# Windowed attention and a feed-forward layer on one core: how Q and K loads, V loads and token blocks are lined up

## The chip, the cores and the metric

The kernel runs on one core of a Trainium2 chip. Its engines work side by side, each with its own in-order list of instructions: TensorE (PE, with its weight loads shown apart as PEld), VectorE (DVE), ScalarE (ACT), GpSimd (POOL) and SyncE (SP), which here issues all DMA transfers. The metric is the device time of one execution in microseconds (us); lower is better.

## The reference

```python
def _attn_ref(q, k, v):                      # all (8, 8, 576, 64): batch, head, token, dim
    scores = (1.0 / np.sqrt(64)) * np.matmul(q, k.transpose(0, 1, 3, 2))
    mask = np.abs(pos[:, None] - pos[None, :]) <= 32
    scores = np.where(mask, scores, -1000000000.0)
    attn = np.exp(scores - np.max(scores, axis=-1, keepdims=True))
    attn = attn / (np.sum(attn, axis=-1, keepdims=True) + 1e-09)
    return np.matmul(attn, v)

def _moe_ref(x, w_in, w_out, s, b):          # x (4608, 512), w_in (512, 2048), w_out (2048, 512)
    r = np.maximum(x @ w_in, 0.0)
    return (s * (r * r) + b) @ w_out         # out (4608, 512), float32
```

Attention within 32 tokens on either side, for 8 batches of 8 heads, gives 8 x 576 = 4608 rows of 512, and each row goes through a layer of 2048 hidden values.

## The kernel before, in words

**One graph, ordered by a planner.** The kernel records every piece of work as a task with `add`: the engine, the instructions, an assumed cost, what it reads and writes, a key (its due time), and for a transfer a triple `dma=(kind, units, ns per unit)`. `_Graph.plan` then plays the tasks through with these costs: at each step it takes, over all engines, the task that can start first (ties go to the smaller key), and keeps a model of SP's DMA ring, in which transfers are served one after another. The order in which it takes the tasks becomes the fixed order of each engine, and `emit` puts the semaphore waits in. So a changed cost, wait or due time does not only move one instruction: it can reorder all engines, and at run time an engine whose next instruction has to wait lets everything behind it wait.

**Attention.** Batches 0 and 1 are loaded and turned in a special way. From batch 2 on (`later`, `piece`) each batch has three loads on SP's queue (line 752): 512 tokens of Q (1 MB), 512 tokens of K (1 MB), and the last 64 tokens of both together. Each lands in a pair of staging buffers `stg` and is cast to bf16 `nat` in two halves (line 760); from batch 3 on, half 0 is POOL's and half 1 DVE's. DMA transposes (line 767) then bring `nat` to `qt` and `ktr`, and POOL copies `ktr` to `kt` in the order wanted (line 777). V comes in units of 128 tokens (`load_v`, line 582, into `vst`) and is cast to `vb` (`cast_v`, line 591, on DVE from batch 2 on). A batch is 4.5 such units. For unit u, PE makes the scores (line 811), ACT the exponentials `ex` (839), DVE multiplies them by the mask (843), PE multiplies by V one unit later, with the row sums (869), in one step together with the next unit's scores, DVE takes reciprocals `rec` (893) and makes the normalised rows `xn` (895), and PE (902) with ACT (910), or later in the kernel a DMA transpose (919), bring these to `xt`, the input of the layer.

What paces the loads: `paced(b, u)` makes a load of batch b wait until a certain attention step of an earlier batch is done. Besides that, the Q and K loads of batch 3 and later wait until the last V load of the batch before has landed (lines 792 and 793).

**The layer.** The 4608 tokens are cut into blocks (`sizes`, line 341): 224, 128, 160, 256, 256 and then 512 each. For each block, `s1` (lines 1113 to 1135) multiplies by `w_in` (PE, line 1124), applies ReLU on ACT (1131) and squares on DVE into `gt` (1133). A group of `s1` fills one accumulator of 512 columns: one chunk of hidden values for a block of 512, two for a block of 256 (`group`). `s2` (line 1142) multiplies 128 tokens of `gt` by `w_out`, in four steps of four matmuls; DVE scales the result to `outs` (1158) and SP writes it (1162). A block's squares must be ready before its `s2`; its `xt` must be ready before its `s1`. Due times of attention units (`due`) are worked out from the block in which their tokens lie, and those of the blocks from a running sum of assumed PE times.

Of the kernel before, what the change touches and what calls it, by code (L numbers as in the profile page):

```python
# [21 lines left out]
PAIRS = 2  # L22
# [25 lines left out]
PACE = ((-1, -1, -1),) * 3  # L48
CASTS = 40.0
LATE = 8  # L50
# [31 lines left out]
class _Graph:  # L82
# [13 lines left out]
    def add(self, stream, fns, cost, reads=(), writes=(), key=0.0, accum=False, dma=None, waits=(),  # L96
            lat=None, slack=0.0):
        if not isinstance(fns, list):
            fns = [fns]
        after = [self.chain] if key < -100 and self.chain else []  # L100
        t = _Task(len(self.tasks), stream, fns, cost, self.LAT[stream] if lat is None else lat, key,
                  dma, slack, after)
        t.deps.update(waits)
        for a in after:
            assert a.stream == stream
            a.next.append(t)
        for r in reads:
            assert r in self.writer, r
            t.deps.add(self.writer[r])
        for w in writes:  # L110
            if w in self.writer:
                t.deps.add(self.writer[w])
            if not accum:
                t.deps.update(self.readers.get(w, ()))
        t.deps.discard(t)
        for r in reads:
            self.readers.setdefault(r, []).append(t)
        for w in writes:
            self.writer[w] = t
            if not accum:  # L120
                self.readers[w] = []
        self.tasks.append(t)
        if key < -100:
            self.chain = t
        return t
# [201 lines left out]
def bass_sliding_window_symmetric__then__act_starrelu_kernel(  # L327
# [10 lines left out]
    B = q.shape[0]  # L338
    T = B * S

    sizes = [224, 128, 160, 256, 256]
    NE = 3
    while sum(sizes) < T:
        sizes.append(min(512, T - sum(sizes)))
# [6 lines left out]
    with ExitStack() as es:  # L351
        uid = {"n": 0}

        def seq_of(b):
            return min(b, LONG)
# [97 lines left out]
        def group_of(b):  # L453

            if b < LONG:
                return range(NUNIT)
            u0 = (NTILE * (b - LONG)) // 2
            return range(u0, (NTILE * (b + 1 - LONG) + (b == B - 1)) // 2)
# [75 lines left out]
        land = {}  # L534

        def pieces(lo, hi, step):
            return range(lo // step, (hi - 1) // step + 1)

        def take(what, n):
            ring[what] += 1  # L540
            return (ring[what] - 1) % n
# [19 lines left out]
        def paced(b, u):  # L561

            c, v = seq_of(b - 1), group_of(b - 1)[0] + u
            while v < 0:
                c, v = c - 1, v + NUNIT
            return land["av", c, v]

        def late(b):

            return "sp" if b < LATE else "act"  # L570
# [166 lines left out]
        def q_later(b):  # L737
            return QTS[b % 2].rearrange("p (i a) s -> p i a s", i=4)

        def piece(b, parts, key, waits):  # L740


            slot = b % 2
            ring["stg"] += ring["stg"] % 2
            ring["nat"] += ring["nat"] % 2
            si, _ = take("stg", NSTG), take("stg", NSTG)
            ni, _ = take("nat", NNAT), take("nat", NNAT)
            stg = STGS[:, si:si + 2, :].rearrange("p x c -> p (x c)")
            nat = NATS[:, ni:ni + 2, :].rearrange("p x c -> p (x c)")
            stgr, natr = [("STG", si), ("STG", si + 1)], [("NAT", ni), ("NAT", ni + 1)]  # L750
            top = max(p0 + n // 4 for _, _, n, p0 in parts)
            add(late(b), [lambda e, name=name, t0=t0, n=n, p0=p0: e.dma_start(
                stg[p0:p0 + n // 4, :].rearrange("p (h c) -> p h c", h=H),
                src_of[name][b, :, t0:t0 + n, :].rearrange("h (p i) d -> p h (i d)", i=4))
                for name, t0, n, p0 in parts],
                500.0 * len(parts), writes=stgr, key=key - 20.0, waits=waits,
                dma=("l", sum(n for _, _, n, _ in parts) // 8, 68.0 if late(b) == "sp" else 61.0))
            for x in (0, 1):
                eng = CASTE[min(b, 3) - 2][x]
                add(eng, lambda e, x=x: e.tensor_copy(  # L760
                    nat[0:top, 1024 * x:1024 * x + 1024].rearrange("p (i h d) -> p h i d", h=H, i=2),
                    stg[0:top, :].rearrange("p (h i d) -> p h i d", h=H, i=4)[:, :, 2 * x:2 * x + 2, :]),
                    110 + (0.53 if eng == "dve" else 1.05) * 1024, reads=stgr, writes=[("NAT", ni + x)], key=key + CASTS, slack=SLACK[0])
            for name, t0, n, p0 in parts:
                np_, s0, xs = n // 4, t0 // 4, pieces(t0, t0 + n, 64)
                dst = q_later(b)[:, :, :, 16 + s0:16 + s0 + np_] if name == "q" else KTR[slot][:, :, :, s0:s0 + np_]
                add("sp", lambda e, dst=dst, p0=p0, np_=np_: e.dma_start(
                    dst.rearrange("p i a s -> p (i a) s"), nat[p0:p0 + np_, :], transpose=True),
                    2000.0 if n > 64 else 1200.0, reads=natr,
                    writes=[("QT", slot, x, pr) for x in xs for pr in range(NPAIR)] if name == "q" else [("KTR", slot, t0)],  # L770
                    key=key + 0.1, dma=("t", np_, 20.0))
                if name == "q":
                    continue
                land["kt", b, t0] = g.tasks[-1]
                for c in range(t0, t0 + n, 128):
                    w = min(128, t0 + n - c)
                    add("pool", lambda e, c=c, w=w: e.tensor_copy(  # L777
                        KT[slot][:, :, c:c + w].rearrange("p a (s i) -> p a s i", i=4),
                        KTR[slot][:, :, :, c // 4:(c + w) // 4].rearrange("p i a s -> p a s i")),
                        100 + 5.5 * w, reads=[("KTR", slot, t0)],  # L780
                        writes=[("KT", slot, x, pr) for x in pieces(c, c + w, 64) for pr in range(NPAIR)],
                        key=key + 3.0, slack=SLACK[1])

        def later(b, key):
            slot = b % 2
            if b < 4:
                for c0, x in ((0, 0), (160, WIN + S)):
                    add("pool", lambda e, c0=c0: e.memset(QTS[slot][:, :, c0:c0 + 16], 0.0), 400,
                        writes=[("QTZ", slot, x)] + [("QT", slot, x, pr) for x in range(NTILE) for pr in range(NPAIR)],
                        key=key - 20.0)  # L790
            for i, parts in enumerate(((("q", 0, 512, 0),), (("k", 0, 512, 0),), (("q", 512, 64, 0), ("k", 512, 64, 32)))):
                piece(b, parts, key + 0.01 * i, [paced(b, PACE[min(b, 4) - 2][i])] +
                      ([land["v", seq_of(b - 1), group_of(b - 1)[-1]]] if b > PAIRS or LATE == PAIRS else []))

# [227 lines left out]
        def attention():  # L1024
# [60 lines left out]
            for b in range(PAIRS, B):  # L1085
                c = seq_of(b)
                later(b, due(c, group_of(b)[0]) - 24.0)
                for i, u in enumerate(group_of(b)):
                    load_v(c, u, due(c, u) - 35.0, late(b), [paced(b, PACEV[min(b, 4) - 2][i])])
                    cast_v(c, u, due(c, u) - 4.0, EV2[i], SLACK[3])  # L1090
                for u in group_of(b):
                    unit(c, u)
                    yield closed[0]
# [381 lines left out]
```

## Time and profile before

| | us |
|---|---|
| three runs | 314.92, 315.22, 316.3 |
| median | 315.22 |
| the profiled execution, its own time | 317.31 |
| its span, first to last instruction | 315.5 |
| PE busy in the span | 296.7 |
| DMA: share of 16 engines' time taken by the data queue | 75.5% |

The granted TensorE clock was 1.0 throughout. In rows of a timeline the columns are: start in us from the span's start, length in us, engine (SPq is SP's queue of DMA issues), line of the kernel, operation, what is written and read, count, and in brackets the idle time before it and what ended it. Lengths of matmuls overlap: the start of the next one tells how long PE was taken. In rows of busy time by stage, each engine's busy time is followed by its number of instructions, and the last three columns are the granted clock, the share of DMA and GB/s.

### The profile page before, as it was taken

To read this page: it belongs to the slowest core of one execution; us is meant where nothing else is said; L and a number is where in the kernel's file an instruction comes from. 1 tells how busy PE (TensorE), PEld (TensorE's weight loads), DVE (VectorE), ACT (ScalarE), POOL (GpSimd) and SP (SyncE) were. 2 spreads that over 40 slices of the span, in tenths; PEclk is the share of its full clock that TensorE was granted. 3 is DMA by queue.
4 is the path that set the end of the run, shared out by engine and by line. 5 is a ranking of instruction groups with operands and counts; after the bars stand their busy time and mean duration, and the time that the engine had idled before them with its cause. 6 is when DMAs were issued, how large, how long until landed. Compare 5 with 4: busy or idle time off the path is not lost.

```text
span 315.5 us, 7901 instructions
## 1 busy us (share of the span) xinstructions
PE 296.7 (94%) x3304; PEld 160.6 (51%) x3348; DVE 195.5 (62%) x387; ACT 141.9 (45%) x224; POOL 93.0 (29%) x110
## 2 busy tenths in 40 slices
PE   7788989999979998999999999999999999999996
PEld 3367756577734544544444444444444444444444
DVE  4678476876596777888577687766445543333312
ACT  4755425356525773654255346444444333333300
POOL 5468854671236235131613241260000000000000
PEclk9999999999999999999999999999999999999999
DMA  6999999997998998799999999996221110000022
GB/s 198 331 386 386 372 251 218 218 199 246 236 188 205 294 140 166 219 225 169 175 318 157 161 221 336 165 154 162 64 59 50 52 46 33 35 34 34 36 91 80
DMA packets 100055, 56.10 MB, mean 178 GB/s; under 512 B 72048, under 2 KB 91248, under 8 KB 100016
## 3 DMA queue, kind: packets, MB, share of 16 engines
q1 hardware_dynamic: 100016, 55.56, 75.5%
q8 instruction: 27, 0.44, 0.6%
q14 instruction: 12, 0.10, 0.1%
HBM read 36.70 MB, written 9.44 MB: 146 GB/s over the span
## 4 chain that ended last, share of the span: by engine, by line
PE 68%; DMA 19%; DVE 6%; issue 3%; SPq 2%; POOL 1%; ACT 0%; POOLq 0%
PE o L1142 30%; PE w L1124 28%; DMA stg<-in_k_dram 10%; DMA stg<-in_moe_w_out_dram 3%; PE avn L869 3%; DMA stg<-in_moe_w_in_dram 3%; DVE gt L1133 2%; PE avn L1173 2%; DMA stg<-in_q_dram 2%; PE sc L811 1%; PE o L1173 1%; DMA vst<-in_v_dram 1%; SPq L667 1%; DVE xn L895 1%; DVE nat L760 1%
## 5 line engine op out<-in xcount | busy, mean ns | idle before, releaser
L1124 PE MATMUL w<-xt,win 128*128 128x512 bf16 (+4 forms) x749 | 140.2, 324 | 3.0 <-ACT r L1131 1.4
L1131 ACT ACTIVATE r<-w 128x512 bf16<-128x512 f32 (+2 forms) x148 | 86.6, 586 | 107.1 <-PE w L1124 91.3
L1142 PE MATMUL o<-wout,gt 128*128 128x512 bf16 (+1 forms) x510 | 123.1, 372 | 2.0 <-issue 1.4
L1133 DVE TENSOR_TENSOR gt<-r 128x512 bf16<-128x512 bf16 (+2 forms) x148 | 79.9, 545 | 72.3 <-ACT r L1131 71.9
L1124 PEld LDWEIGHTS w<-xt,win 128*128 128x128 bf16 x768 | 68.3, 98 | 54.0 <-DVE kt L711 0.9
L1142 PEld LDWEIGHTS o<-wout,gt 128*128 128x128 bf16 x528 | 50.6, 98 | 54.6
L760 POOL CAST nat<-stg 128x1024 bf16<-128x1024 f32 (+1 forms) x21 | 26.7, 1271 | 60.7 <-DMA stg<-in_q_dram 37.6
L777 POOL COPY kt<-ktr 128x512 bf16<-128x512 bf16 (+1 forms) x30 | 31.6, 1054 | 38.5 <-DMA ktr<-nat 37.1
L839 ACT ACTIVATE ex<-sc 128x1024 bf16<-128x1024 f32 (+1 forms) x28 | 28.7, 1023 | 23.2 <-PE avn L869 22.4
L1158 DVE SCALAR_TENSOR_TENSOR outs<-o,sb,cvec 128x512 f32<-128x512 f32 (+1 forms) x35 | 25.4, 729 | 14.2 <-PE o L1142 14.0
L895 DVE TENSOR_TENSOR xn<-avn,rec 128x512 bf16<-128x512 f32 (+1 forms) x31 | 21.4, 689 | 1.1 <-DVE rec L893 0.2
L843 DVE TENSOR_TENSOR ex<-ex,mask 128x1024 bf16<-128x1024 bf16 (+1 forms) x28 | 21.2, 758 | 1.0 <-ACT ex L839 0.2
L869 PE MATMUL avn<-vb,ex 64*64 64x65 bf16 x944 | 19.9, 197 | 1.5 <-issue 1.3
L869 PEld LDWEIGHTS avn<-vb,ex 64*64 64x64 bf16 x944 | 12.9, 106 | 14.5 <-issue 8.7
L760 DVE CAST nat<-stg 128x1024 bf16<-128x1024 f32 (+1 forms) x15 | 11.1, 740 | 7.2 <-DMA stg<-in_k_dram 5.1
L591 DVE CAST vb<-vst 128x512 bf16<-128x512 f32 (+1 forms) x28 | 13.7, 494 | 0.0
L811 PE MATMUL sc<-qt,kt 64*64 64x128 bf16 x432 | 11.3, 216 | 0.0
L910 ACT COPY xt<-avn 128x512 bf16<-128x512 bf16 (+2 forms) x14 | 7.1, 516 | 8.1 <-PE avn L902 8.1
L893 DVE RECIPROCAL rec<-avn 128x8 f32<-128x8 f32 (+1 forms) x31 | 6.2, 201 | 5.9 <-PE avn L869 5.5
L557 POOL CAST win<-stg 128x1024 bf16<-128x1024 f32 x8 | 8.4, 1056 | 3.7 <-DMA stg<-in_moe_w_in_dram 3.6
L557 POOL CAST wout<-stg 128x1024 bf16<-128x1024 f32 x8 | 9.0, 1122 | 1.7 <-DMA stg<-in_moe_w_out_dram 1.0
L1173 PE MATMUL o<-wout,gt 128*128 128x512 bf16 x29 | 8.2, 379 | 1.0 <-POOL wout L557 0.9
(119 smaller groups left out, 146.1 us busy)
## 6 DMA issues: line engine op xcount, KB each, us to landing
out_dram<-outs SPq DMA_DIRECT2D x35, 256.0 KB, 2.5
vst<-in_v_dram SPq DMA_DIRECT2D x28, 256.0 KB, 5.2
stg<-in_k_dram SPq DMA_DIRECT2D x6, 1024.0 KB, 11.1
stg<-in_q_dram SPq DMA_DIRECT2D x6, 1024.0 KB, 6.6
stg<-in_moe_w_in_dram SPq DMA_DIRECT2D x8, 512.0 KB, 9.2
stg<-in_moe_w_out_dram SPq DMA_DIRECT2D x8, 512.0 KB, 9.6
stg<-in_q_dram SPq DMA_DIRECT2D x8, 256.0 KB, 5.4
stg<-in_k_dram SPq DMA_DIRECT2D x8, 256.0 KB, 5.4
```

The lines of the kernel that those rows point to most:

```text
L760: add(eng, lambda e, x=x: e.tensor_copy(nat[0:top, 1024 * x:1024 * x + 1024].rearrange("p (i h d) -> p h i d", h=H, i=2), stg[0:top, :].re ...
L777: add("pool", lambda e, c=c, w=w: e.tensor_copy(KT[slot][:, :, c:c + w].rearrange("p a (s i) -> p a s i", i=4), KTR[slot][:, :, :, c // 4: ...
L839: add("act", lambda e, dst=flat_dst, src=flat_src: e.activation(dst, src, AF.Exp, bias=0.0, scale=0.125), 190 + 0.833 * 512 * len(hs), rea ...
L843: add("dve", lambda e, flat=flat, mask=mask: e.tensor_tensor(flat, flat, mask, ALU.mult), 130 + 0.53 * 512 * len(hs), reads=[("E", ei, hp, ...
L869: return [lambda e: e.matmul(av[64 * x:64 * x + 64, h, 0:D + 1], lhsT=buf[64 * g:64 * g + 64, h % 2, h // 2, c:c + 64], rhs=VB[64 * g:64 * ...
L895: add("dve", lambda e: e.tensor_tensor(XN[xi][0:p1, :].rearrange("p (a c) -> p a c", a=H), av[0:p1, :, 0:D], REC[ri][0:p1, :].rearrange("p ...
L1124: add("pe", [lambda e, g=g, kc=kc: e.matmul(wt[:, g, :], lhsT=WIN_BF[:, kc, (f0 + g) * 128:(f0 + g + 1) * 128], rhs=XT[:, kc, t0 % XR:t0 % ...
L1131: add("act", lambda e: e.activation(rt, wt, AF.Relu, bias=0.0, scale=1.0), 190 + 0.833 * ng * nt, reads=[("W", wb)], writes=[("R1", rb)], ...
L1133: add("dve", lambda e: e.tensor_tensor(GT[gs][:, f0:f0 + ng, g0:g0 + nt], rt, rt, ALU.mult), 130 + 0.53 * ng * nt, reads=[("R1", rb)], wri ...
L1142: add("pe", [lambda e, fc=fc: e.matmul(O[:, ob, 0:cn], lhsT=GT[gs][:, fc, g0:g0 + 128], rhs=WOUT_BF[:, fc, c0:c0 + cn], start=(fc == 0), s ...
L1158: add("dve", lambda e: e.scalar_tensor_tensor(OUTS[us][:, 0:cn], bank, SB128[:, 0:1], CVEC[:, c0:c0 + cn], ALU.mult, ALU.add), 200 + 1.07 ...
L1173: add("pe", [lambda e, fc=fc, bank=bank, gs=gs, g0=g0: e.matmul(bank, lhsT=GT[gs][:, fc, g0:g0 + 128], rhs=WOUT_BF[:, fc, :], start=(fc == ...
```

## The change

Three edits. The block of tokens 1024 to 1535 becomes two blocks of 256, so that there are 13 blocks in place of 12. The planner counts 74 ns in place of 68 for each of the 64 units of a large Q or K load (and of the 16 of the small one). And the wait of Q and K loads for the last V load of the batch before is taken away; their pacing stays. Since lines go, the changed kernel's numbers after line 792 are one lower (869 becomes 868, 1124 becomes 1123).

```diff
-    sizes = [224, 128, 160, 256, 256]
+    sizes = [224, 128, 160, 256, 256, 256, 256]
...
-                dma=("l", sum(n for _, _, n, _ in parts) // 8, 68.0 if late(b) == "sp" else 61.0))
+                dma=("l", sum(n for _, _, n, _ in parts) // 8, 74.0 if late(b) == "sp" else 61.0))
...
             for i, parts in enumerate(((("q", 0, 512, 0),), (("k", 0, 512, 0),), (("q", 512, 64, 0), ("k", 512, 64, 32)))):
-                piece(b, parts, key + 0.01 * i, [paced(b, PACE[min(b, 4) - 2][i])] +
-                      ([land["v", seq_of(b - 1), group_of(b - 1)[-1]]] if b > PAIRS or LATE == PAIRS else []))
+                piece(b, parts, key + 0.01 * i, [paced(b, PACE[min(b, 4) - 2][i])])
```

In the changed kernel's order, the first difference on SP is that the third V load of batch 2 stands before that batch's K transpose instead of behind it, and its fourth and fifth stand behind the Q and K loads of batch 3. On PE, the `s1` groups of tokens 1024 to 1279 stand between steps that were `s2` steps alone.

## Prediction

> **What bounds the kernel now.** I read the page first (busy shares, the chain that ended last), then busy time by stage, then the timeline of TensorE (PE) for its gaps, and for each gap the timelines of the engine it waited for and of SyncE's queue (SP). From the page, busy time by engine and the chain's shares by engine:
>
> ```profile
> PE 296.7 (94%) x3304; PEld 160.6 (51%) x3348; DVE 195.5 (62%) x387; ACT 141.9 (45%) x224; POOL 93.0 (29%) x110
> PE 68%; DMA 19%; DVE 6%; issue 3%; SPq 2%; POOL 1%; ACT 0%; POOLq 0%
> ```
>
> PE is the bound, but a fifth of the chain is DMA. Busy time by stage (columns: stage, length, busy of PE, weight loads, DVE, ACT, POOL) says where PE still loses time:
>
> ```profile
> 60.00:89.00 29.00, 27.14 (x401) 19.68 (x407) 21.30 (x40) 15.78 (x26) 13.73 (x13) 1.00 1.00 216
> 89.00:120.00 31.00, 28.59 (x387) 14.66 (x382) 24.42 (x46) 18.17 (x28) 10.24 (x9) 1.00 1.00 204
> 120.00:226.00 106.00, 103.41 (x1194) 51.06 (x1209) 76.25 (x146) 50.53 (x76) 32.60 (x29) 1.00 0.99 195
> ```
>
> Before 60 us nothing is touched by the change. After 120 us PE's timeline shows gaps of 0.16 us alone, and each stands before a row of 3, 7 or 11 matmuls where 4, 8 or 12 were issued: a record is missing, not time. Between 60 and 120 us there are exactly two real holes. The PE timeline (start, length, line, work, count, idle before):
>
> ```profile
> 79.19 1.04 PE L1124 MATMUL w<-xt,win 128*128 128x256 bf16 x8
> 80.06 1.03 PE L1142 MATMUL o<-wout,gt 128*128 128x512 bf16 x4
> ...
> 86.47 1.03 PE L1142 MATMUL o<-wout,gt 128*128 128x512 bf16 x4
> 88.77 0.32 PE L869 MATMUL avn<-vb,ex 64*64 64x65 bf16 x16 [1.27 <-issue]
> ...
> 117.10 1.03 PE L1142 MATMUL o<-wout,gt 128*128 128x512 bf16 x4
> 119.42 0.40 PE L902 MATMUL avn<-ident,xn 128*128 128x128 bf16 x4 [1.30 <-DVE xn L895]
> ```
>
> Four 512-column matmuls take 0.865 us from start to start (late in the run such groups start at 294.91, 295.78 and 296.64), so PE was free at 87.33 and at 117.97: the holes cost 1.44 and 1.45 us, 2.9 together. What DVE did then:
>
> ```profile
> 86.53 0.69 DVE L760 CAST nat<-stg 128x1024 bf16<-128x1024 f32 x1 [1.85 <-DMA stg<-in_k_dram]
> 87.14 1.52 DVE L843 TENSOR_TENSOR ex<-ex,mask 128x1024 bf16<-128x1024 bf16 x1
> ...
> 114.55 0.69 DVE L760 CAST nat<-stg 128x1024 bf16<-128x1024 f32 x1 [1.69 <-DMA stg<-in_k_dram]
> 115.16 1.26 DVE L1133 TENSOR_TENSOR gt<-r 128x512 bf16<-128x512 bf16 x1
> 116.34 1.52 DVE L760 CAST nat<-stg 48x1024 bf16<-48x1024 f32 x1
> ...
> 118.67 0.69 DVE L895 TENSOR_TENSOR xn<-avn,rec 128x512 bf16<-128x512 f32 x1
> ```
>
> Both holes are one story: DVE stands idle at its cast of a K load that has not landed (batch 3, then batch 4), and behind that cast in its order wait the mask product or the normalised rows that PE needs. POOL's two casts of the same K start with it (86.56, 3.00 us), and beside them the mask product takes 1.52 us instead of its usual 0.69. The chain of waits runs through K's loads, 11.47 us from 75.04 and 13.16 us from 101.37. SP's queue shows why they began when they did:
>
> ```profile
> 70.57 0.63 SPq L582 DMA_DIRECT2D vst<-in_v_dram  x1
> 71.25 3.14 SPq L1162 DMA_DIRECT2D out_dram<-outs  x4
> 74.49 0.51 SPq L752 DMA_DIRECT2D stg<-in_q_dram  x1
> 75.04 0.89 SPq L752 DMA_DIRECT2D stg<-in_k_dram  x1
> ...
> 97.80 0.57 SPq L582 DMA_DIRECT2D vst<-in_v_dram  x1
> 98.42 1.55 SPq L1162 DMA_DIRECT2D out_dram<-outs  x3
> 100.93 0.39 SPq L752 DMA_DIRECT2D stg<-in_q_dram  x1
> ```
>
> The V load of 97.80 landed 3.07 us later, at 100.87, and Q was issued at 100.93: that is the wait which the change removes.
>
> **The wait removed.** In the changed order batch 3's Q and K stand ahead of batch 2's fourth and fifth V loads; the third V goes ahead of the batch's K transpose. So two V issues leave SP's path to Q: half of the 1.20 us pair at 63.21 and the 0.63 us at 70.57, 1.25 us (the third V fits into the 1.8 us that SP had before the transpose of 59.99). K lands at 86.51 - 1.25 = 85.3. The DVE order after it is unchanged (cast, mask product), so PE gets its operand 2.26 us after K, as before (88.77 - 86.51): 87.55, against PE free at 87.33. **Hole 1 shrinks from 1.44 to 0.2 us**; 0 to 0.9 if the shift is 1.5 or 0.6.
>
> What pays: the two V loads now land behind batch 3's small Q/K load (1.6 us after K in the trace): 86.9, plus some 0.65 each as between two V loads at 67.6 and 68.3, gives 87.6 and 88.3. DVE casts the first of them right after the reciprocal (0.20) and product (0.69) that follow the attention step of 87.55, so not before 89. The cover is 1.5 us.
>
> From batch 4 on, the V loads whose landing was waited for still stand before Q and K in SP's order; only the wait goes, and Q is then held by its pacing on an attention step of two batches back. That needs the second part.
>
> **Two blocks of 256.** The same columns in 64 more matmuls and 64 more weight loads; ACT's and DVE's instructions keep count and shape (two 256-column chunks share one 128x512 instruction). Eight 256-column matmuls start to start: 79.19 to 80.06, 0.87 us, against 0.865 for four of 512; over 16 groups 0.1 us, at most 0.3 from the spread of such rows (0.87 to 0.88). One weight load is 98 ns and hides behind a 109 ns matmul. **+0.1 us.** [...]
>
> What the split buys is order: the first half needs attention only up to token 1279, so its matmuls can start some 10 us earlier, between the steps that wait for DVE, and the attention steps move back. Between hole 1's step and the step that paces batch 4's Q, the new PE order has 14 groups of 0.865 us, the old 10: 3.5 us more work. So this step comes at 99.68 + 3.5 - 1.2 (hole closed) = 102.0, ends at 102.7, and Q of batch 4 goes out then, 1.8 us *later* than now, but with the three outputs of 98.42 already gone from the ring. K needs 12.0 us from Q's issue as in batch 3 (13.6 as in batch 4 now): 114.7, at most 116.3.
>
> From that step to hole 2's transposes the new order has 15 groups, 3 transposes of 0.23 and 3 attention steps of 0.79: 16.1 us, so PE asks for its rows at 102.8 + 16.1 = 118.9. DVE after K: cast, square, reciprocal, small cast, product. By the rows of now the small cast ends 3.3 us after K (117.86 - 114.53); 0.2 and 0.69 more give 4.3 us with the hand-over: 119.0. **Hole 2 shrinks from 1.45 to 0.1 us**; 1.45 or slightly more if K takes 13.6 us. Between, and nearer the first since the ring is free: 0.4.
>
> **The planner's 74.** No instruction is added. It thinks each large load longer by 64 x 6 ns = 0.4 us, so DVE's casts stand later in the order: at hole 2 the small cast now has one square and one reciprocal before it instead of one square, and two squares fewer stand between it and the rows PE wants. Real loads (81.19 to 86.51, 5.3 us) are longer still than the 4.7 it now counts, so some lateness stays; later batches had it too and showed no hole. Nothing, within 0.3 us either way.
>
> **Sum.** 2.9 lost now, 0.2 + 0.4 left, 0.1 for the matmuls: -2.2 us. Span 315.5 to 313.3; the profiled execution's own 317.3 to 315.1 (1.8 us lie around the span). The median of the three runs shown is 315.22, 2.1 below that execution; what it does without is not seen. Taking the saving over whole gives 313.0, and a little less, 313.1, since these runs may have smaller holes.
>
> **Rivals.**
> - *The holes stay or are smaller without the profiler.* For: the median lies 2.1 us below the profiled execution; batch 4's Q is still paced, and goes out later. If half of 2.9 us is not there to save, or hole 2 returns, the gain is 0.8: 314.4. Chance 0.24.
> - *V becomes the late one (slower).* DVE is in order, so a V cast that waits stops squares, masks and rows alike. It decides when batch 2's fourth V lands after about 89, that is when the large loads in front take over 1.5 us more than assumed. One such stall costs what hole 1 did, and the shifted pacing repeats it in the batches after: 3 x 1.4 - 2.2 = 2 us, 317.2. Against: V transfers are short (0.65 us) and every V after batch 2 keeps its place. Chance 0.09.
> - *Weight loads bound the 256-column matmuls.* 64 extra loads of 98 ns uncovered: +6.3 us, 319.3. Against: 128 such matmuls run at 109 ns already. [...] Chance 0.02.
> - *More goes than the two holes.* Both holes at zero and no cost: 312.3. That is the floor, as PE has no other gap after 60 us.
>
> **Numbers.** Forecast as summed 0.65, the rivals 0.24, 0.09 and 0.02. A difference under 0.5% (1.6 us) is about what a measurement of this kernel can tell from none. The forecast's own range, 312.3 to 314.0, is mostly beyond that line (313.6); I put faster at 0.63, within 0.5% at 0.27, slower 0.10. The range 312.2 to 315.8 takes in the first rival and leaves out the slower ones.
>
> **What would show it.** Right: no idle over 0.5 us before the attention step near 87 us and before the transposes near 119 us in PE's timeline; 256-column rows x8 at 0.87 us between 87 and 118 us; Q of batch 3 issued near 73.2 and of batch 4 near 102.7; K landing at 85.3 and near 115. Wrong: DVE's cast of V idle for DMA (L591) with PE waiting behind it, a hole of over 1 us left at batch 4, or new holes after 120 us.

## The result, and the profile after

| | before | after |
|---|---|---|
| median, 21 runs each on the same chip | 315.76 us | 317.51 us |
| lowest and highest | 314.04, 318.97 | 316.3, 321.4 |
| ratio after to before, 95% interval | | 1.0072 [1.0051, 1.0093] |
| the profiled execution: own time, span | 317.31, 315.5 | 319.59, 317.7 |

The changed kernel is slower by 0.7%, about 2.3 us by the ratio, which leaves out one run of each kernel in a slower state; the medians lie 1.75 us apart. Forecast were 313.1 us, in a range of 312.2 to 315.8.

From the page of the changed kernel: busy time by engine, the granted clock in 40 slices, the queue of instruction packets (queue, packets, MB, share) and the shares of the chain that ended last:

```profile
PE 305.7 (96%) x3412; PEld 169.2 (53%) x3412; DVE 197.4 (62%) x387; ACT 141.7 (45%) x224; POOL 90.3 (28%) x110
PEclk9699999999999997999999999999999999999999
q8 instruction: 28, 0.46, 0.6%
PE 83%; DMA 10%; DVE 2%; issue 2%; POOL 1%; SPq 1%; ACT 0%; POOLq 0%
```

DMA fell from 19% to 10% of the chain and PE rose from 68% to 83%: the waits that the forecast wanted to remove did go. PE's 305.7 us can't be held against the 296.7 of before, where 44 of 3348 matmul records are missing. But the clock row has a 7 in the slice near 119 us, where before had 9 throughout. The queue q8, called "instruction", moved 27 packets before and 28 here; 0.46 MB in 28 packets is 16 KB each. In fourteen profiles of this case (all but the wait alone and the 74 alone) it is 28 with the split's extra matmuls and 27 without, so it is taken here for the queue that brings PE's own program.

PE's timeline at the place of the first hole, and around the second:

```profile
86.55 1.04 PE L1123 MATMUL w<-xt,win 128*128 128x256 bf16 x8
87.43 1.03 PE L1141 MATMUL o<-wout,gt 128*128 128x512 bf16 x4
88.38 0.32 PE L868 MATMUL avn<-vb,ex 64*64 64x65 bf16 x16
...
115.77 0.32 PE L868 MATMUL avn<-vb,ex 64*64 64x65 bf16 x16
115.92 0.39 PE L810 MATMUL sc<-qt,kt 64*64 64x128 bf16 x16
116.17 0.31 PE L868 MATMUL avn<-vb,ex 64*64 64x65 bf16 x13
118.47 0.22 PE L868 MATMUL avn<-vb,ex 64*64 64x65 bf16 x3 [2.00 <-issue]
118.63 1.59 PE L1123 MATMUL w<-xt,win 128*128 128x256 bf16 x8
120.01 1.91 PE L1141 MATMUL o<-wout,gt 128*128 128x512 bf16 x4
121.72 1.37 PE L1123 MATMUL w<-xt,win 128*128 128x256 bf16 x8
122.92 0.39 PE L901 MATMUL avn<-ident,xn 128*128 128x128 bf16 x4
```

Near 87 us there is no idle left (0.88 us from a row of eight to the next, then 0.95). Near 116 us stands something new: PE stops for 2.00 us *inside* one task, after 13 of its 16 matmuls, though a task's waits stand ahead of its first one; nothing is named as what ended the wait ("issue"). Behind it three groups take 1.38, 1.71 and 1.20 us from start to start in place of 0.88, 0.865 and 0.88. The busy time from 118.90 to 122.50 shows why (its last three columns are clock, DMA share and GB/s):

```profile
118.90:122.50 3.60, 3.60 (x17) 1.99 (x15) 2.23 (x5) 1.46 (x2) 0.00 (x0) 0.53 1.05 155
```

The clock was at half for 3.41 us, from 118.97 by its records. DVE, which the old holes waited for, is on time at both places, and the second place shows PE as the late one:

```profile
85.55 0.68 DVE L760 CAST nat<-stg 128x1024 bf16<-128x1024 f32 x1
86.15 1.52 DVE L842 TENSOR_TENSOR ex<-ex,mask 128x1024 bf16<-128x1024 bf16 x1
...
118.74 0.21 DVE L892 RECIPROCAL rec<-avn 128x8 f32<-128x8 f32 x1 [1.29 <-PE avn L868]
```

SP's queue, to be held against the forecast's issue times:

```profile
71.90 0.57 SPq L752 DMA_DIRECT2D stg<-in_q_dram  x1
72.51 1.78 SPq L752 DMA_DIRECT2D stg<-in_k_dram  x1
...
77.05 3.36 SPq L582 DMA_DIRECT2D vst<-in_v_dram  x2
...
103.24 0.40 SPq L752 DMA_DIRECT2D stg<-in_q_dram  x1
```

So of the two profiled executions: 2.9 us of holes gone; 2.00 us for the stop, 0.50, 0.85 and 0.32 us for the three groups behind it (each against its usual start to start), 0.3 at a late square near 186 us and 0.16 for the split come in. From the first 256-column group after 60 us to the layer's last weight load PE took 251.5 us, against 250.2 before. The other 0.95 us of the span lie before that group, where the clock row of after has a 6 near 10 us (half clock from 9.75 us for 6.83 us, by its records); the change touches nothing there.

### The profile page after: what moved, and what is told of

Its sections match the earlier page's. It is cut to its first block, busy times and chain, and to the rows that moved or that the text cites. A ratio compares the mean times of both kernels' runs of the same rounds, so it can differ in the third digit from the quotient of the medians.

```text
span 317.7 us, 8058 instructions
## 1 busy us (share of the span) xinstructions
PE 305.7 (96%) x3412; PEld 169.2 (53%) x3412; DVE 197.4 (62%) x387; ACT 141.7 (45%) x224; POOL 90.3 (28%) x110
## 4 chain that ended last, share of the span: by engine, by line
PE 83%; DMA 10%; DVE 2%; issue 2%; POOL 1%; SPq 1%; ACT 0%; POOLq 0%
PE w L1123 36%; PE o L1141 35%; PE avn L868 4%; DMA stg<-in_moe_w_out_dram 3%; DMA stg<-in_moe_w_in_dram 3%; DMA stg<-in_k_dram 2%; DMA stg<-in_q_dram 2%; PE sc L810 2%; PE avn L1172 2%; PE o L1172 1%; SPq L667 1%; DVE gt L1132 1%; PE avn L901 1%; PE sc L943 0%; DVE kt L711 0%
## 5 line engine op out<-in xcount | busy, mean ns | idle before, releaser
L1123 PE MATMUL w<-xt,win 128*128 128x512 bf16 (+4 forms) x832 | 144.8, 315 | 0.2
L1141 PE MATMUL o<-wout,gt 128*128 128x512 bf16 (+1 forms) x528 | 126.7, 375 | 0.3 <-DVE gt L1132 0.3
L1123 PEld LDWEIGHTS w<-xt,win 128*128 128x128 bf16 x832 | 74.7, 98 | 50.9 <-DVE kt L711 0.9
L760 POOL CAST nat<-stg 128x1024 bf16<-128x1024 f32 (+1 forms) x21 | 24.7, 1174 | 59.0 <-DMA stg<-in_q_dram 36.2
L842 DVE TENSOR_TENSOR ex<-ex,mask 128x1024 bf16<-128x1024 bf16 (+1 forms) x28 | 20.3, 723 | 1.7 <-ACT ex L838 0.5
L760 DVE CAST nat<-stg 128x1024 bf16<-128x1024 f32 (+1 forms) x15 | 11.8, 784 | 0.0
L705 PE MATMUL w<-ident,nat 128*128 128x128 bf16 x64 | 7.0, 255 | 3.3 <-DVE nat L692 2.6
L1172 PE MATMUL avn<-wout,gt 128*128 128x512 bf16 x32 | 9.2, 381 | 0.0
```

The lines of the kernel that those rows point to most:

```text
L760: add(eng, lambda e, x=x: e.tensor_copy(nat[0:top, 1024 * x:1024 * x + 1024].rearrange("p (i h d) -> p h i d", h=H, i=2), stg[0:top, :].re ...
L842: add("dve", lambda e, flat=flat, mask=mask: e.tensor_tensor(flat, flat, mask, ALU.mult), 130 + 0.53 * 512 * len(hs), reads=[("E", ei, hp, ...
L1123: add("pe", [lambda e, g=g, kc=kc: e.matmul(wt[:, g, :], lhsT=WIN_BF[:, kc, (f0 + g) * 128:(f0 + g + 1) * 128], rhs=XT[:, kc, t0 % XR:t0 % ...
L1141: add("pe", [lambda e, fc=fc: e.matmul(O[:, ob, 0:cn], lhsT=GT[gs][:, fc, g0:g0 + 128], rhs=WOUT_BF[:, fc, c0:c0 + cn], start=(fc == 0), s ...
L1172: add("pe", [lambda e, fc=fc, bank=bank, gs=gs, g0=g0: e.matmul(bank, lhsT=GT[gs][:, fc, g0:g0 + 128], rhs=WOUT_BF[:, fc, :], start=(fc == ...
```

## The experiments

Ratios are against the kernel before, run on the same chip beside each kernel. The theories at the outset: (A) the split costs, through PE's instructions or clock; (B) the new order of the loads costs; (C) the forecast was right in kind.

### One part at a time

The split alone, on the kernel before:

```diff
-    sizes = [224, 128, 160, 256, 256]
+    sizes = [224, 128, 160, 256, 256, 256, 256]
```

> The kernel before with the split into two blocks of 256 alone. Theory A (the split: 128 more PE instructions in the stretch where PE already runs through its list fastest; PE waits for its own instructions, as for 2.00 us at 116.48 in the trace after, and the clock halves behind it): slower than before by 1.5 to 3 us, and in the trace a gap of over 1 us on PE between 88 and 125 us that no engine or transfer ends. Theory B (the order of the loads, wait removed): within 1 us of before. Theory C (the forecast was right in kind and only later stages pay): faster by about 1 us.

Measured: 320.99 us, ratio 1.013 [1.0078, 1.0182].

The changed kernel without the split (`sizes` as before, the other two edits kept):

> The changed kernel with the block of 512 back: no wait for V, 74 ns, no split. Theory A: at or below the time before (0 to 2 us faster), since one or both of the DVE holes near 87 and 118 us close and PE has as many instructions as before. Theory B: slower by 1.5 to 3 us, as the whole change. Theory C: faster by about 1 us.

Measured: 315.27 us, ratio 1.0002 [0.997, 1.0034].

The wait alone, on the kernel before:

```diff
-                piece(b, parts, key + 0.01 * i, [paced(b, PACE[min(b, 4) - 2][i])] +
-                      ([land["v", seq_of(b - 1), group_of(b - 1)[-1]]] if b > PAIRS or LATE == PAIRS else []))
+                piece(b, parts, key + 0.01 * i, [paced(b, PACE[min(b, 4) - 2][i])])
```

> The kernel before with only the wait for V taken away. Theory A: within 1 us of before. Theory B: slower by 1 to 3 us, with DVE idle at a cast of V or K and PE waiting behind it. Theory C: Q and K land up to 1.3 us earlier, faster by 0 to 1 us.

Measured: 317.95 us, ratio 1.0049 [1.0008, 1.009]. The planner's 74 in place of 68 alone:

> The kernel before with only the planner's 74 ns in place of 68. Theory A and B: DVE's casts of Q and K stand later in its order, so the holes near 87 and 118 us shrink: 0 to 2 us faster. Theory C: about 0.3 us either way.

Measured: 315.4 us, ratio 0.9983 [0.9952, 1.0015].

What follows: the split costs about 2.2 us beside the other two edits (ratios 1.0072 and 1.0002), and the other two together are worth nothing. None of the four beats the kernel before, though holes of over 1.4 us are absent in the profiles of two of them (the last two edits together, and the 74 alone). Their PE timelines show where time is lost, first the split alone and then the wait alone:

```profile
217.18 0.32 PE L869 MATMUL avn<-vb,ex 64*64 64x65 bf16 x16 [1.81 <-POOL kt L777]
...
218.85 1.91 PE L1142 MATMUL o<-wout,gt 128*128 128x512 bf16 x4
220.56 1.72 PE L1124 MATMUL w<-xt,win 128*128 128x512 bf16 x4
```

```profile
87.84 0.40 PE L901 MATMUL avn<-ident,xn 128*128 128x128 bf16 x4 [1.58 <-DVE xn L894]
...
178.50 0.32 PE L868 MATMUL avn<-vb,ex 64*64 64x65 bf16 x16 [2.04 <-POOL kt L777]
```

Each has stops of its own, at other places and with other causes (a K that lands late for DVE, a K transpose that comes late for POOL), and in the first the clock goes to half again (four 512-column matmuls in 1.71 us). That raised two questions: do such stops belong to a kernel or to an execution, and what is the stop that nothing ends?

### Moving PE's program without changing its order

PE has 64 more weight loads and matmuls after the split, and one packet more. If the stop inside a task is PE waiting for its own program, it must move when the program is shifted against its packets. Eight, 24, 40 or 80 tiny matmuls (16 x 16) behind the warm-up do that; where there are 40 or 80, the five warm-up matmuls of 512 columns become four or two. The orders of all engines stay the same otherwise. For 40:

```diff
-                                      start=True, stop=True)] * WARM,
+                                      start=True, stop=True)] * 4 + [lambda e: e.matmul(W[0:16, 1, 0:16], lhsT=ONESW[0:64, 0:16], rhs=ONESW[0:64, 0:16], start=True, stop=True)] * 40,
```

> The changed kernel with one of its five warm-up matmuls on PE replaced by 40 tiny ones (16 rows, 16 columns; about as long in all), so that every later PE instruction stands some 78 places later in PE's program; all engines' orders are otherwise the same. Supply theory: PE stops in the middle of an attention step at 116 us because the next 16 KB packet of its own program came late, and where packets begin against the data transfers is chance. Then the 2.0 us stop at 116 us moves or goes, and with it the 3.4 us of half clock behind it: up to 3.7 us off the changed kernel's 317.5, 313.8 to 316; it can also meet another transfer and stay at 317 to 318. Order theory: the loss lies in the order of the work, and a shift does nothing: 317.5 within 0.5, stop at the same instruction.

Measured: 315.52 us, ratio 1.0002 [0.9978, 1.0026]; no stop near 116 us.

> The same with three warm-up matmuls replaced by 80 tiny ones: some 154 places later. Supply theory: a third setting of the packets, with a time of its own between 313.8 and 319, and stops of PE without a releaser at another instruction than in the changed kernel. Order theory: 317.5 within 0.5.

Measured: 316.51 us, ratio 1.0023 [0.9992, 1.0053]; PE has no stop over 0.6 us after 60 us, but two stretches of 3.41 us at half clock, from 16.58 and 23.41 us; whether the shortened warm-up brings them is not shown.

The kernel before with 40 such matmuls:

> The kernel before with the same 40 tiny matmuls. Supply theory: this kernel too has a time that hangs on the setting, so it differs from the kernel before by 0.5 to 2 us in one direction or the other. Order theory: ratio 1.000 within 0.002, and the two holes at 87 and 118 us are there again (1.4 us each), as they come from K's landing.

Measured: 317.51 us, ratio 1.0055 [1.0029, 1.0082]. The order theory's 1.000 is out, but what its timeline shows are late operands, not a stop inside a task:

```profile
89.32 0.32 PE L869 MATMUL avn<-vb,ex 64*64 64x65 bf16 x16 [1.90 <-issue]
...
146.06 0.32 PE L869 MATMUL avn<-vb,ex 64*64 64x65 bf16 x16 [1.64 <-DVE ex L843]
```

At both places DVE had waited for a K load again (2.48 us until 87.09, 1.92 us until 141.50). This is one execution, and the kernel before has such holes in one execution and not in others (below), so it doesn't show that the shift brought them. All twelve runs lie above the median of the kernel before (315.99 us and more against 315.09), so some part belongs to the shift, by a way that stays open; of the program's packets this run shows nothing.

The split's extra matmuls without its new order (`sizes` as before):

```diff
-                       for g in range(ng) for kc in range(4)],
+                       for g in range(ng) for kc in range(4)] if t0 != 1024 else [lambda e, h=h, kc=kc: e.matmul(wt[:, 0, h:h + 256], lhsT=WIN_BF[:, kc, f0 * 128:(f0 + 1) * 128], rhs=XT[:, kc, t0 % XR + h:t0 % XR + h + 256], start=(kc == 0), stop=(kc == 3)) for h in (0, 256) for kc in range(4)],
```

> The two other edits, with the block of 1024 to 1535 kept at 512 tokens in the plan, but its 64 matmuls of 512 columns issued as 128 of 256 each; orders of all engines as without the split. Count theory (64 more pairs of weight load and matmul, and the packets that they move, are what the split costs): 317 to 318, 2 us over the 315.3 of the kernel without the split. Order theory (the split costs by the place to which it moves groups and attention steps): 315.3 to 315.6, as the prediction's term of 0.1 us has it.

Measured: 316.13 us, ratio 1.002 [0.999, 1.005], between the two expectations. Its profile does not lie between: with the order of the kernel that has no split, and no such stop there, it has one at nearly the same place:

```profile
115.25 0.28 PE L868 MATMUL avn<-vb,ex 64*64 64x65 bf16 x9
116.69 0.25 PE L868 MATMUL avn<-vb,ex 64*64 64x65 bf16 x7 [1.16 <-issue]
```

So the stop comes with the extra instructions and not with the split's new order. They are not enough by themselves, though: the split alone has as many and has no such stop.

### The same two kernels profiled again

> The kernel before, unchanged, looked at once more. Forecast's reading (the two holes at 87 and 118 us belong to the kernel): both are there again at 1.2 to 1.6 us each, span near 315.5. Chance theory (they belong to that one execution, and the median of 315.1 is of executions without them): span 313 to 314, idle of PE after 60 us under 1 us in all, K loads of batches 3 and 4 landing up to 2 us earlier.

> The same a third time: by the chance theory at least one of the two new looks lacks both holes; by the forecast's reading both looks have them.

Measured: own times 314.29 and 316.52 us, spans 312.6 and 314.8. PE at both places, in the first of these executions:

```profile
86.50 1.03 PE L1142 MATMUL o<-wout,gt 128*128 128x512 bf16 x4
87.45 0.32 PE L869 MATMUL avn<-vb,ex 64*64 64x65 bf16 x16
...
115.75 1.03 PE L1142 MATMUL o<-wout,gt 128*128 128x512 bf16 x4
116.61 0.39 PE L902 MATMUL avn<-ident,xn 128*128 128x128 bf16 x4
```

Neither hole is there. The second execution has none near 88 us and 0.51 us of idle near 118. K's large loads differ: batch 4's took 13.16 us in the execution that the forecast was made from, and 10.02 and 12.24 us in these; batch 3's took 11.47, then 10.36 and 10.22. The holes belong to an execution in which two loads were slow.

> The changed kernel, unchanged, looked at once more. Supply theory: PE's program has the same packets, so the stop of 2.0 us at the 13th of 16 matmuls of the attention step near 116 us is there again, with half clock behind it or without; span 315 to 318. Chance theory: it is gone in this look, and stops of another kind are there.

> The same a third time: the supply theory expects the stop near 116 us in both new looks, the chance theory in none or one.

Measured: 316.34 and 315.14 us. The stop is there in both, at the same matmul:

```profile
114.49 0.31 PE L868 MATMUL avn<-vb,ex 64*64 64x65 bf16 x13
116.33 0.22 PE L868 MATMUL avn<-vb,ex 64*64 64x65 bf16 x3 [1.53 <-issue]
```

```profile
115.06 0.31 PE L868 MATMUL avn<-vb,ex 64*64 64x65 bf16 x13
116.36 0.22 PE L868 MATMUL avn<-vb,ex 64*64 64x65 bf16 x3 [0.99 <-issue]
```

The records of the instruction packets point to its cause. In the three profiled executions of the changed kernel a packet began at 115.56, 113.61 and 113.61 us, 0.2 to 1.1 us before the attention step, and took 1.31, 1.22 and 1.24 us. PE came to its stop 45 to 48 weight loads later and went on 1.60, 1.50 and 1.51 us after the packet had ended; in the kernel with halved matmuls, 48 and 1.53. And in all four the stop stands behind exactly 1649 records of PE's queue other than matmuls (in the first execution 1616 weight loads, 32 semaphore records and one drain), though in the halved kernel's order that is another matmul of the step: that speaks for the place in the program. The step's 45 short matmuls before the stop took only 0.7 us in the first execution, which agrees with PE having run through what it had of its program before the rest was there; no record shows that wait itself. In the split alone the packet came as late (after 1597 such records), but longer matmuls followed, PE reached the 1649 at 120.57 us, 2.68 us after the packet's end at 117.89, and there was no stop. What fills the 1.5 us between a packet's end and PE's next instruction the records don't show; in the third execution of the changed kernel PE came to its stop only after the packet had ended.

### Where exactly

> The changed kernel with 8 tiny matmuls behind the warm-up, so that all later PE instructions stand 16 places later in their packets. In three looks at the changed kernel PE came to a stop 45 to 48 pairs of weight load and matmul after the fetch of a packet had begun, at the 13th of the last 16 matmuls of an attention step, and went on 1.50 to 1.60 us after that fetch had ended. Run-out theory (PE ate up what it had of its program; the 45 short pairs before the packet's end take only 0.9 us): the stop comes 8 pairs earlier in the step, at the 5th of the last 16 matmuls, and is 0.5 to 0.9 us shorter if the fetch starts those 8 pairs earlier among 256-column matmuls, or is gone if the fetch then lies ahead of the wait that opens the step. Order theory (the step's own operands stop it): the stop stays at the 13th.

Measured: 314.97 us, ratio 0.9981 [0.9942, 1.0019].

> The same with 24: run-out theory: the packet's end lies 24 pairs earlier, with some 24 pairs of 109 ns before it in place of short ones, 2.6 us, so the stop is under 0.3 us or gone and the median lies 1 to 2 us under the changed kernel's 317.5, at 315.3 to 316.5. Order theory: stop and median as in the changed kernel.

Measured: 316.22 us, ratio 1.0015 [0.9979, 1.005]. PE at the place with 8 extra matmuls:

```profile
115.53 0.32 PE L868 MATMUL avn<-vb,ex 64*64 64x65 bf16 x16
115.69 0.39 PE L810 MATMUL sc<-qt,kt 64*64 64x128 bf16 x16
115.93 0.32 PE L868 MATMUL avn<-vb,ex 64*64 64x65 bf16 x16
116.18 1.05 PE L1123 MATMUL w<-xt,win 128*128 128x256 bf16 x8
```

The step runs through. The packet now began at 111.17 us, and at 110.80 with 24: more than 4 us ahead of the step, with 27 recorded matmuls between the two from 111.73 and 111.78 us on, where the first execution of the changed kernel had no weight load between them. Eight instruction pairs of no use, at the start of the program, took 2.5 us off the changed kernel's median (0.9981 against 1.0072 by the ratios). This was the second branch of the run-out theory (the fetch lies ahead of the wait that opens the step). Why a packet's fetch comes so late in the unshifted program, in the first execution 218 weight loads after the one before it, where 3412 in 28 packets make 122 on the mean, is not shown: PE's reading held back by that wait, or the packet's turn among the data transfers, are guesses that would both fit. That it began after 1604, 1604 and 1601 records of PE's queue in the three executions speaks for a place in the program, and so for the first.

## Why the prediction was wrong

**The holes.** Gone at both places, as said. Q of batch 3 was issued at 71.90 (73.2 forecast) and K landed at 84.05 (85.3); Q of batch 4 at 103.24 (102.7), K at 113.64 (114.7). For batch 3 this is the forecast's mechanism: the load took 11.54 us against 11.47, and landed earlier as it was issued earlier. For batch 4 it took 9.97 us in place of 13.16; since the kernel before needed 10.02 and 12.24 in other executions, how much of that the change brought is not shown. None of the seven profiled executions of the changed kernel, shifted or not, has either hole, and the sum of 2.9 us was right for the execution of the forecast. The step that failed is "taking the saving over whole" to the median of the runs: the holes belonged to that execution, and in the two others of the same kernel nothing of them is left but 0.51 us. In those there was next to nothing to save. From the first 256-column group to the layer's last weight load PE took 250.2 us in the execution of the forecast, 247.3 and 248.0 in the two others, and 247.1 to 247.7 in the changed kernel with its program shifted. So the execution of 314.29 us already stood where both holes at zero lead (250.2 less 2.9 is 247.3); the fourth rival's floor of 312.3 takes the holes off a median that, by these executions, hardly had them. How many executions have them isn't known; only 3 of the 21 runs of before took longer than the 317.31 us of the one profiled. Nor do the holes explain every long time: the execution of 316.52 us began this stretch 1.3 us later than the others (63.27 against 61.94 and 61.96).

**The first rival** saw this gap and priced it at half of the holes. Its reason was off: the profiler does not bring the holes, since two profiled executions are without them; the slow loads of one execution did. And it still ended at a gain.

**The split.** The term of 0.1 us for the matmuls is right as far as it goes: 256-column rows x8 follow each other in 0.88 us, and the rival of uncovered weight loads (319.3) did not occur. The term that was missing is the instructions themselves. The prediction counted 64 matmuls and 64 weight loads by their durations, not by the place they take in PE's program. One stop costs 1.0 to 2.0 us in each of three profiled executions, half clock behind it 1.7 us more in one of them; the stretch named above took 251.5, 249.9 and 248.3 us there. That is of the size of the 2.3 us measured, and with the stop shifted away the ratios are 0.9981, 1.0002, 1.0015 and 1.0023, all with 1 in their intervals: the change without the stop is worth nothing that can be measured. How much of the 2.3 us is the stop is not measured to the end, as a shift can cost by itself (1.0055 on the kernel before).

**V becoming the late one.** It did not: DVE's casts of V (line 591) had no idle before them, in either kernel's page (28 casts, 0.0 us). The fourth and fifth V of batch 2 landed at 86.27 and 86.68 us (87.6 and 88.3 forecast). The slower side came by another way.

**The planner's 74.** Nothing within 0.3 us was forecast; alone it measured 0.9983 [0.9952, 1.0015], which agrees.

**Left open.** The wait alone measured 1.0049, with stops at K's landing and at POOL's copy in its one profiled execution, and the split alone 1.013, with stops of 1.09, 1.01 and 1.81 us and none at its program's packets. Whether these belong to the kernels or, like the holes of before, to an execution, one execution each can't say; that all their runs lie above the median of the kernel before speaks for a part that stays. The half clock stood behind one of the changed kernel's three stops near 116 us, so its share in the median isn't known.

## What to carry to other kernels

If the profiled execution is slower than the median of the runs by about as much as its holes are long (here 2.1 us against the three runs shown at first, and 2.9 us), profile a second execution before planning to remove them: two further executions of the kernel before had neither of the two holes, but for 0.51 us. On PE, busy for 94 to 96% of the span here, the 128 added instructions came with more than their own durations: three profiled executions have a stop of 0.99 to 2.00 us inside a run of very short matmuls (45 in 0.7 us), and four with the program moved by 8 to 80 tiny matmuls have none there. An edit worth under 1% should therefore be measured with a few harmless instructions more or less at the start (8 took the ratio from 1.0072 to 0.9981 here), and a stop inside a task, with nothing named that ended it, is the mark to look for.

## What the hardware showed beside that

**PE stopped inside a task.** The stops were 0.99 to 2.00 us in the changed kernel's three executions and 1.16 us in the kernel with halved matmuls. The 0.46 MB of the queue came in 28 packets of 16 KB. At this place 45 matmuls went by in 0.7 us and a packet took 1.2 to 1.3 us; in the split alone PE came there 2.68 us after the packet's end, and did not stop. That it was the program PE waited for is the author's reading of the packets and the shifts.

**Half clock followed some stops of about 2 us.** In the changed kernel half clock began at 118.97 us, 0.50 us after the stop of 2.00 us, and lasted 3.41 us. After the stop of 1.81 us in the split alone the mean clock was 0.51 from 218.50 to 222.00 us, and after that of 1.90 us in the kernel before with 40 extra matmuls 0.51 from 90.30 to 93.75 us: again some 3.4 us at half clock. None followed the stop of 2.04 us in the wait alone (178.50 us), whose clock was 1.000 on the mean of the span, nor those of 1.53 and 0.99 us in the changed kernel's two other executions (0.999 and 1.000). So the length of a stop did not decide it alone. Nor does half clock need such a stop: the 6.83 us from 9.75 us in the changed kernel's first execution had no idle of PE over 0.84 us in the 3.41 us before them. What decides it is not shown.
